# Attention, feed-forward and mixture kernel: transposes of a tile three steps behind its scores, weighted sums eight steps behind

## The chip, the cores and the metric

One core of one Trainium2 chip runs the whole program. The metric is device time in microseconds of one execution; the kernel before takes 1406.84 us (median of 3 runs, 1406.71 to 1406.88).

## The reference

Three stages follow one another; all inputs are float32. Attention has 2 batches of 8 heads, 768 positions of 64 numbers each; a position sees the first 4 positions (the sinks) and the last 128 including itself. The two later stages work on the 1536 x 512 matrix that comes out of it.

```
# attention, for each batch and head
scores = q @ k.T / 8;  scores = where(sink or in window, scores, -1e9)
a = exp(scores - max(scores));  a = a / (a.sum(-1) + 1e-9);  x = a @ v
# feed-forward: d_ff = 2048
h = x @ w_in;  x = (h * sigmoid(h)) @ w_out
# mixture: 8 experts of 1024, P from eight row and column normalisations
P = sinkhorn(exp(x @ w_gate - max));  out = sum_e P[:, e] * (relu(x @ w1[e]) @ w2[e])
```

## The kernel before

Every large product is made of three passes over high and low parts of the operands (`three`, lines 110 to 113): high by high, high by low, low by high. A high part is a copy in the matmul's number format, made by ScalarE (or GpSimd for the values); the low part is what it leaves, made by a subtraction on VectorE or GpSimd.

The attention stage is the function `banded`. Two heads of a batch form a unit; there are 8 units. A unit has 6 query tiles of 128 positions, so there are 48 tiles, numbered s. Three tiles form a window w of 384 positions, of which there are 16. The instructions are issued in the order that the loop over steps writes out (line 325), and each engine works through its own in this order. The loop has 57 steps, numbered s; ii is the step's place in its group of three. In step s the loop issues, in this order:

- `scores(s)`: for two heads, queries by keys on TensorE (L236) into one bank of PSUM each, out of three; on VectorE the mask, and the negative row maximum in one operation (L240). In the first 8 steps four transposes without use follow (L96).
- `exponentials(s - 1)`: for two heads on ScalarE (L248), with the row sums. The results lie in one of 7 buffers `pr`.
- one part of `weighted`: three parts make up a window's sums, values by transposed tiles in three passes (L111 to L113), the first part also with the sinks' high values (L292), the last with their low ones (L302). A part has 6 matmuls of 256 columns, or 12 (first part of a unit's second window). The last part's sum is split into `xH` and `xL`, the input of the next stage.
- `normalise(s - 2)`: on VectorE an addition to the sums (L253), then, behind the low parts (L313) of what the step before had transposed or summed, the reciprocal (L255); on GpSimd two multiplications of the tile by it, one for each head (L257).
- `turn(s - 4)`: two or four transposes of the normalised tile on TensorE (L270), into one of three banks; when ii is 0, `turn_sinks(w - 2)`: three more for a window's sinks (L280).
- high parts of what the step transposed or summed, on ScalarE (L308).
- one piece of the split of the unit's values on GpSimd (`values`, L222 and L224), the loads of later units, and then one step of the generator `timeline` (line 992).

The generator `timeline` brings work of the next stage into these steps: the first weight blocks, which come as 64-bit floating-point numbers, are decoded in eight halves (lines 527 to 555: on ScalarE L535, L545 and L554, on VectorE L540, L541 and L543, on GpSimd L536, L547, L548 and L555). Once the 48 scores are issued it puts blocks of the first layer (twelve matmuls of 512 columns, `first`, lines 626 to 640) into some of the nine last steps: steps 48 to 51 and 54 to 56. The blocks from step 54 on need the sums of window 14. The remaining blocks follow the loop.

Of the kernel before, what the change touches and what calls it, by code (L numbers as in the profile page):

```python
# [26 lines left out]
def attn_ffn_moe_kernel(ctx, tc, q, k, v, n_sink, window, w_in, w_out, w_gate, w1, w2, out):  # L27
# [3 lines left out]
    NT = S // 128  # L31
# [19 lines left out]
    NU = len(units)  # L51
# [42 lines left out]
    def warm_up(ps, n):  # L94
        for _ in range(n):
            nc.tensor.transpose(ps[:, 0:128], ident, ident)  # L96
# [13 lines left out]
    def three(ps, sH, sL, mH, mL, first, last, **kw):  # L110
        nc.tensor.matmul(ps, sH, mH, start=first, stop=False, **kw)  # L111
        nc.tensor.matmul(ps, sH, mL, start=False, stop=False, **kw)  # L112
        nc.tensor.matmul(ps, sL, mH, start=False, stop=last, **kw)  # L113
# [35 lines left out]
    def banded(sp, experts):  # L149
# [36 lines left out]
        def masks():  # L186
            nc.vector.tensor_scalar(kp[:, prev], it[:, prev], wd, None, ALU.is_lt)
            nc.vector.tensor_scalar(mk[:, 1, own], kp[:, own], -1.0, -NEG, ALU.add, ALU.mult)
            nc.vector.tensor_tensor(mk[:, 1, prev], kp[:, prev], snk, ALU.max)
            yield  # L190
            nc.vector.tensor_scalar(mk[:, 1, prev], mk[:, 1, prev], -1.0, -NEG, ALU.add, ALU.mult)
            yield
            nc.vector.tensor_copy(kp[:, 128 : 128 + SK], snk[:, 0:SK])
            nc.vector.tensor_scalar(mk[:, 2], kp, -1.0, -NEG, ALU.add, ALU.mult)
# [49 lines left out]
        def exponentials(s):  # L244
            pr = prs[s % 7]
            sm = sp.small.tile([128, 2], F32, name=f"sm{s}", tag="sm")
            for h, (ng, nm) in enumerate(logits.pop(s)):
                nc.scalar.activation(pr[:, :, h], ng, AF.Exp, bias=nm, scale=-1.0, accum_out=sm[:, h : h + 1])  # L248
            probs[s] = (pr, sm)
# [9 lines left out]
        def turn(s):  # L259

            i = s % NT
            g = i // 3
            pr = probs[s][0]
            js = [(0, 0)] if i == 0 else [(i - 1, 0), (i, 160)]
            n = len(js)
            ps = sp.bank(f"tp{s}", "tr")
            for h in range(2):
                for m, (j, k0) in enumerate(js):
                    o = 128 * (n * h + m)
                    nc.tensor.transpose(ps[:, o : o + 128], pr[:, k0 : k0 + 128, h], ident)  # L270
            ws = [where[j, i] for j, _ in js]
            d = slice(ws[0], ws[-1] + 1, max(ws[-1] - ws[0], 1))
            return [(pt[g][0][:, :, d], pt[g][1][:, :, d], ps[:, : 256 * n].rearrange("p (h m c) -> p h m c", h=2, m=n))]

        def turn_sinks(w):
            ss = sss[w % 2]
            ps = sp.bank(f"ts{w}", "tr")
            for ii in range(3):
                pr = probs.pop(3 * w + ii)[0]
                nc.tensor.transpose(ps[:64, 128 * ii : 128 * ii + 128], pr[:, 128:160, :].rearrange("p s h -> p (s h)"), ident)  # L280
            sinks[w] = ss
            return [(ss[0:64], ss[64:128], ps[0:64, :384])]

        def weighted(w, part):

            u, g = divmod(w, 2)
            b, hp = units[u]
            pH, pL = pt[g]
            ms = [[[0], [1], [2]], [[0, 1], [2], [3]]][g][part]
            if part == 0:  # L290
                pos[w] = sp.bank(f"pv{w}", "pv")[:, :384]
                nc.tensor.matmul(pos[w], vs[0][:, u], sinks[w], start=True, stop=False)  # L292
            po = pos[w]
            for m in ms:
                j, t0 = prods[g][m]
                for h in range(2):
                    vH, vL = (x[:, j, 64 * h : 64 * h + 128] for x in vz[u % 2])
                    mH, mL = (x[:, h, 2 * m : 2 * m + 2].rearrange("p a b -> p (a b)") for x in (pH, pL))
                    three(po[:, 128 * t0 : 128 * t0 + 256], vH, vL, mH, mL, False, False, skip_group_check=True)
            if part < 2:  # L300
                return []
            nc.tensor.matmul(po, vs[1][:, u], sinks.pop(w), start=False, stop=True)  # L302
            c = slice(b * S + 384 * g, b * S + 384 * g + 384)
            return [(xH[hp][:, c], xL[hp][:, c], pos.pop(w))]
# [6 lines left out]
        def lows(parts):  # L311
            for o, l, i in parts:
                nc.vector.tensor_tensor(l, i, f32(o), ALU.subtract)  # L313
# [7 lines left out]
        NS = NT * NU  # L321
        late = []
        vals = iter(())
        setup = masks()
        for s in range(NS + 9):
            w, ii = divmod(s, 3)
            parts, late = late, []
            if s < NS:
                scores(s)
            if s < 8:  # L330
                warm_up(sp.bank("wt", "tr"), 4)
            next(setup, None)
            next(setup, None)
            if 0 <= s - 1 < NS:
                exponentials(s - 1)
            if s >= 9:
                late += weighted((s - 9) // 3, ii)
            nrm = normalise(s - 2) if 0 <= s - 2 < NS else iter(())
            next(nrm, None)
            lows(parts)  # L340
            next(nrm, None)
            if 0 <= s - 4 < NS:
                late += turn(s - 4)
            if ii == 0 and 0 <= w - 2 < 2 * NU:
                late += turn_sinks(w - 2)
            highs(late)
            if s >= NS:
                lows(late)
                late = []
            if s in (3, 4):  # L350
                c = slice(4 * s - 12, 4 * s - 8)
                nc.scalar.copy(vs[0][:, c], vsr[:, c])
                nc.gpsimd.tensor_tensor(vs[1][:, c], vsr[:, c], f32(vs[0][:, c]), ALU.subtract)
            if (s == 4 or s > 2 and s % 6 == 2) and s // 6 < NU:
                vals = values(s // 6)
            next(vals, None)
            if s % 6 == 0 and 0 < s and s // 6 + 1 < NU:
                load_unit(s // 6 + 1, "kq")
            if (s == 8 or s > 5 and s % 6 == 5) and s // 6 + 2 - (s == 8) < NU:
                load_unit(s // 6 + 2 - (s == 8), "v")  # L360
            next(experts)
# [611 lines left out]
    with tc.If(rvl != 0) as cmp:  # L973
        with tc.manual_schedule(), ExitStack() as st:
            sp = Space(st)
            ex = Experts(sp)
            ex.plan(True)

            halves = [words(sp.vsr, 512 * i, 512) for i in range(2)]
            tmp = [[words(sp.tm, 512 * i + 256 * c, 256) for c in range(2)] for i in range(2)]  # L980

            def load_half(i):
                c = 256 * (i // 2)
                nc.sync.dma_start(halves[i % 2].bitcast(I32).rearrange("p (k f) -> p k f", k=2), w_in.bitcast(I32)[:, c : c + 256].rearrange("(k p) f -> p k f", p=128)[:, 2 * (i % 2) : 2 * (i % 2) + 2])

            def decode_half(i):
                o = [words(t, 256 * (i % 2), 256, F32R) for t in ex.buffer("A", 0, i // 2)]
                yield from ex.decode(halves[i % 2], tmp[i % 2], o, True)
                if i + 2 < 8:
                    load_half(i + 2)  # L990

            def timeline():
                gens = {}
                for s in range(NT * NU + 9):
                    if s == 5:
                        load_half(0)
                        load_half(1)
                    for i in range(8):
                        at = s - 7 - 5 * i
                        if at == 0:  # L1000
                            gens[i] = decode_half(i)
                        if at in (0, 1, 2, 3, 4, 5, 6):
                            next(gens[i], None)
                    at = s - NT * NU
                    for a in (-6, -1, -1, 0):
                        if at == a:
                            ex.fetch()
                    if at == -3:
                        gens["Z"] = ex.prepare("Z", 0, 0)
                    if -3 <= at <= 1:  # L1010
                        next(gens["Z"], None)
                    if at in (0, 1, 2, 3, 6, 7, 8):
                        next(blocks)
                    yield

            blocks = ex.run(True)
            banded(sp, timeline())
            sp.cycle = ["sc"] * 3 + ["tr"] * 3
            for _ in blocks:
                pass  # L1020
# [51 lines left out]
```

## Time and profile before

| | before |
|---|---|
| median of 3 runs | 1406.84 us |
| profiled execution, its own time | 1406.43 us |
| its span, first to last instruction | 1404.5 us |
| busy: TensorE, VectorE, ScalarE, GpSimd | 1394.5, 850.8, 538.2, 504.3 us |
| granted TensorE clock, mean | 0.999 |
| attention stage, scores of the first to those of the last tile | 8.59 to 118.10 us |

The profile records one execution. The table's busy times are unions of the instructions' durations; those of matmuls overlap and their ends are modelled, so the distance between starts says more than a duration. The stage around the change is the first tenth of the span; the two later stages take the rest, in which TensorE is busy nearly all the time.

### The profile page before, as it was taken

The page shows a single profiled execution, that of the slowest core. Times are in us where ns is not written, and L with a number is a line of the kernel's source. Part 1 is how long each engine was busy: PE and PEld are TensorE (multiplying, and loading weights), DVE is VectorE, ACT ScalarE, POOL GpSimd, SP SyncE. Part 2 cuts the span into 40 slices and gives each one's busy share as a digit, 9 for nine tenths or more (in the row PEclk, how much of TensorE's full clock was granted, in tenths as well). Part 3 has the DMA queues.
Part 4 walks back from the last instruction along what each step waited for, and adds up shares of the span by engine and source line. Part 5 has one row for each costly group of instructions (what it writes and reads, how often), then busy time and mean ns, then how long its engine had stood idle before and what let it go on. Part 6 is the DMA issues. An engine that isn't in the chain of part 4 may idle for free.

```text
span 1404.5 us, 18978 instructions
## 1 busy us (share of the span) xinstructions
PE 1394.5 (99%) x7065; PEld 1221.5 (87%) x7065; DVE 850.8 (61%) x1645; ACT 538.2 (38%) x1241; POOL 504.3 (36%) x657
## 2 busy tenths in 40 slices
PE   8999999999999999999999999999999999999998
PEld 6778888888878998889989998998899889989997
DVE  7988897686566656554555455455545554555454
ACT  6887334333354333333333333333233333332330
POOL 7887232222133333433332234323322333232230
PEclk9999999999999999999999999999999999999999
DMA  5341221211001000011001001100100010001002
GB/s 133 110 129 67 70 83 65 69 60 61 16 25 36 31 31 31 30 45 31 31 31 45 30 31 32 44 31 31 46 31 30 31 45 30 31 31 46 16 0 93
DMA packets 60293, 65.29 MB, mean 46 GB/s; under 512 B 10400, under 2 KB 47520, under 8 KB 60192
## 3 DMA queue, kind: packets, MB, share of 16 engines
q1 hardware_dynamic: 59904, 63.99, 14.3%
q8 instruction: 57, 0.93, 0.3%
q14 instruction: 44, 0.36, 0.1%
q10 hardware_dynamic: 288, 0.00, 0.0%
HBM read 60.84 MB, written 3.15 MB: 46 GB/s over the span
## 4 chain that ended last, share of the span: by engine, by line
PE 97%; POOL 1%; DVE 1%; DMA 1%; SPq 0%; ACT 0%; issue 0%; ACTq 0%; DVEq 0%
PE py L112 12%; PE py L113 12%; PE py L111 12%; PE pq L111 11%; PE pq L113 11%; PE pq L112 11%; PE pz L112 3%; PE pz L111 3%; PE pz L113 3%; PE pa L112 3%; PE pa L113 3%; PE pa L111 3%; PE sc L236 2%; PE tp L270 1%; PE pv L111 1%; PE pv L113 1%
## 5 line engine op out<-in xcount | busy, mean ns | idle before, releaser
L834 DVE SCALAR_TENSOR_TENSOR pr<-py,P,pr 128x512 f32<-128x512 f32 x224 | 168.0, 750 | 117.9 <-PE py L113 117.9
L113 PE MATMUL py<-pt,vz 128*128 128x512 f32 x576 | 225.4, 391 | 0.0
L112 PE MATMUL py<-pt,vz 128*128 128x512 f32 x576 | 225.3, 391 | 0.0
L111 PE MATMUL py<-pt,vz 128*128 128x512 f32 x576 | 224.8, 390 | 0.3 <-DVE ngm L886 0.3
L787 DVE TENSOR_TENSOR mk<-pq,rqk 128x384 f32<-128x384 f32 x128 | 71.3, 557 | 205.3 <-PE pq L113 205.3
L571 POOL TENSOR_TENSOR pt<-ng,pt 128x256 fp32r<-128x256 f32 (+1 forms) x66 | 66.4, 1011 | 211.3 <-ACT pt L570 211.3
L571 POOL TENSOR_TENSOR pt<-rqk,pt 128x512 fp32r<-128x512 f32 (+1 forms) x50 | 55.4, 1108 | 225.1 <-ACT pt L570 225.1
L113 PEld LDWEIGHTS py<-pt,vz 128*128 128x128 f32 x576 | 108.1, 188 | 22.8
L111 PEld LDWEIGHTS py<-pt,vz 128*128 128x128 f32 x576 | 108.1, 188 | 20.7 <-DVE ngm L886 0.3
L112 PEld LDWEIGHTS py<-pt,vz 128*128 128x128 f32 x576 | 108.1, 188 | 19.9
L794 ACT COPY rqk<-pq 128x384 f32<-128x384 f32 x64 | 30.7, 480 | 216.4 <-PE pq L113 216.4
L790 ACT ACTIVATE vz<-mk 128x384 fp32r<-128x384 f32 x128 | 66.9, 522 | 80.0 <-DVE mk L787 80.0
L791 DVE SCALAR_TENSOR_TENSOR vz<-mk,vz 128x384 fp32r<-128x384 f32 x128 | 71.0, 554 | 7.7 <-ACT vz L790 7.7
L112 PE MATMUL py<-pt,ss 128*128 128x512 f32 x192 | 74.9, 390 | 0.0
L111 PE MATMUL py<-pt,ss 128*128 128x512 f32 x192 | 74.6, 389 | 0.0
L636 ACT ACTIVATE mk<-pa 128x512 f32<-128x512 f32 x48 | 28.7, 599 | 89.8 <-PE pa L113 82.1
L834 DVE SCALAR_TENSOR_TENSOR tm<-py,P,tm 128x512 f32<-128x512 f32 x56 | 42.0, 751 | 32.6 <-PE py L113 32.6
L637 DVE TENSOR_TENSOR mk<-mk,pa 128x512 f32<-128x512 f32 x48 | 32.9, 685 | 41.6 <-ACT mk L636 41.6
L570 ACT CAST pt<-ng 128x256 fp32r<-128x256 f32 (+1 forms) x66 | 33.5, 509 | 63.2 <-POOL ng L585 24.9
L257 POOL TENSOR_SCALAR pr<-pr,sm 128x288 f32<-128x288 f32 x96 | 52.1, 560 | 15.4 <-DVE sm L255 6.6
L111 PE MATMUL pa<-xH,wa 128*128 128x512 f32 x144 | 56.4, 392 | 0.0
L112 PE MATMUL pa<-xL,wa 128*128 128x512 f32 x144 | 56.2, 390 | 0.3 <-DVE xL L313 0.3
(428 smaller groups left out, 3799.9 us busy)
## 6 DMA issues: line engine op xcount, KB each, us to landing
rqk<-in_moe_w_dram SPq DMA_DIRECT2D x32, 512.0 KB, 3.3
rv<-in_moe_w_dram SPq DMA_DIRECT2D x16, 512.0 KB, 3.4
ng<-in_moe_w_dram SPq DMA_DIRECT2D x16, 512.0 KB, 3.2
rqk<-in_moe_w_out_dram SPq DMA_DIRECT2D x8, 512.0 KB, 3.3
rv<-in_v_dram SPq DMA_DIRECT2D x8, 384.0 KB, 3.8
rqk<-in_moe_w_in_dram SPq DMA_DIRECT2D x6, 512.0 KB, 3.8
rqk<-in_k_dram SPq DMA_DIRECT2D x7, 384.0 KB, 4.7
rqk<-in_q_dram SPq DMA_DIRECT2D x7, 384.0 KB, 5.1
```

Source lines behind the costliest of these rows:

```text
L111: nc.tensor.matmul(ps, sH, mH, start=first, stop=False, **kw)
L112: nc.tensor.matmul(ps, sH, mL, start=False, stop=False, **kw)
L113: nc.tensor.matmul(ps, sL, mH, start=False, stop=last, **kw)
L257: nc.gpsimd.tensor_scalar(pr[:, :, h], pr[:, :, h], sm[:, h : h + 1], 1.0, ALU.mult, ALU.mult)
L570: nc.scalar.copy(o[0], src)
L571: nc.gpsimd.tensor_tensor(o[1], src, f32(o[0]), ALU.subtract)
L637: nc.vector.tensor_tensor(sg, sg, ps, ALU.mult)
L787: add = lambda o, x, y: nc.vector.tensor_tensor(o, x, y, ALU.add)
L790: nc.scalar.activation(oH, src, AF.Relu)
L791: nc.vector.scalar_tensor_tensor(oL, src, 0.0, f32(oH), ALU.max, ALU.subtract)
L794: nc.scalar.copy(self.p1, ps)
L834: nc.vector.scalar_tensor_tensor(o, ps, self.P[:, tt, e : e + 1], o, ALU.mult, ALU.add)
```

## The change

In the loop over steps the transposes of a tile are issued one step earlier relative to its scores, those of a window's sinks too (in the last step of a group of three, with the window before it, where they stood in the first with the window two before), and the three parts of the weighted sums begin eight steps behind a window's first scores, where they began nine behind. Normalisation keeps its step. The loop has one step less, and `timeline` too; the last three blocks of the first layer that are issued inside it move from the seventh, eighth and ninth of the last steps to the sixth, seventh and eighth.

```diff
-        for s in range(NS + 9):
+        for s in range(NS + 8):
...
-            if s >= 9:
-                late += weighted((s - 9) // 3, ii)
+            if s >= 8:
+                late += weighted(*divmod(s - 8, 3))
             nrm = normalise(s - 2) if 0 <= s - 2 < NS else iter(())
             next(nrm, None)
             lows(parts)
             next(nrm, None)
-            if 0 <= s - 4 < NS:
-                late += turn(s - 4)
-            if ii == 0 and 0 <= w - 2 < 2 * NU:
-                late += turn_sinks(w - 2)
+            if 0 <= s - 3 < NS:
+                late += turn(s - 3)
+            if ii == 2 and 0 <= w - 1 < 2 * NU:
+                late += turn_sinks(w - 1)
...
-                for s in range(NT * NU + 9):
+                for s in range(NT * NU + 8):
...
-                    if at in (0, 1, 2, 3, 6, 7, 8):
+                    if at in (0, 1, 2, 3, 5, 6, 7):
                         next(blocks)
```

## Rows read from the trace of the kernel before

**Rows 1.** Busy time by stretch: per engine, then clock, DMA share, GB/s.
```profile
8.00:28.00 20.00, 18.91 (x113) 11.96 (x111) 17.61 (x73) 13.89 (x45) 16.59 (x33) 1.00 0.67 168
28.00:118.00 90.00, 90.00 (x608) 69.07 (x605) 81.30 (x305) 76.27 (x232) 76.42 (x130) 1.00 0.35 100
```

**Rows 2.** Timeline of TensorE: start us, duration us, engine, line, operation, operands.
```profile
35.65 0.76 PE L236 MATMUL sc<-rqk 64*128 64x288 f32 x4
...
37.72 0.76 PE L236 MATMUL sc<-rqk 64*128 64x288 f32 x4
...
61.47 0.76 PE L236 MATMUL sc<-rqk 64*128 64x288 f32 x4
...
63.87 0.65 PE L270 MATMUL tp<-ident,pr 128*128 128x128 f32 x4
...
64.77 0.76 PE L236 MATMUL sc<-rqk 64*128 64x288 f32 x4
...
66.28 0.64 PE L270 MATMUL tp<-ident,pr 128*128 128x128 f32 x4
66.85 0.76 PE L236 MATMUL sc<-rqk 64*128 64x288 f32 x4
...
69.08 0.76 PE L236 MATMUL sc<-rqk 64*128 64x288 f32 x4
...
71.67 0.76 PE L236 MATMUL sc<-rqk 64*128 64x288 f32 x4
...
73.50 0.76 PE L236 MATMUL sc<-rqk 64*128 64x288 f32 x4
...
75.74 0.76 PE L236 MATMUL sc<-rqk 64*128 64x288 f32 x4
...
117.34 0.76 PE L236 MATMUL sc<-rqk 64*128 64x288 f32 x4
```

**Rows 3.** Timeline of GpSimd, same columns; in brackets idle time before and its releaser.
```profile
36.71 1.05 POOL L257 TENSOR_SCALAR pr<-pr,sm 128x288 f32<-128x288 f32 x2
...
38.89 1.05 POOL L257 TENSOR_SCALAR pr<-pr,sm 128x288 f32<-128x288 f32 x2 [0.65 <-DVE sm L255]
...
63.98 1.15 POOL L257 TENSOR_SCALAR pr<-pr,sm 128x288 f32<-128x288 f32 x2
...
66.23 0.73 POOL L555 TENSOR_TENSOR wa<-tm,wa 128x256 fp32r<-128x256 f32 x1
66.94 1.03 POOL L257 TENSOR_SCALAR pr<-pr,sm 128x288 f32<-128x288 f32 x2
...
76.08 1.30 POOL L257 TENSOR_SCALAR pr<-pr,sm 128x288 f32<-128x288 f32 x2
...
116.82 1.03 POOL L257 TENSOR_SCALAR pr<-pr,sm 128x288 f32<-128x288 f32 x2 [1.32 <-DVE sm L255]
...
123.25 1.03 POOL L257 TENSOR_SCALAR pr<-pr,sm 128x288 f32<-128x288 f32 x2
```

**Rows 4.** Timeline of VectorE in the step that begins at 35.65 us.
```profile
36.43 0.46 DVE L240 CUSTOM_DVE_ANT_0 ng<-sc,mk 128x288 f32<-128x288 f32 x1 [1.04 <-PE sc L236]
...
37.26 0.69 DVE L313 TENSOR_TENSOR pt<-tp,pt 128x512 fp32r<-128x512 f32 x1
37.98 0.55 DVE L313 TENSOR_TENSOR ss<-ts,ss 64x384 fp32r<-64x384 f32 x1
38.56 0.17 DVE L255 RECIPROCAL sm<-sm 128x2 f32<-128x2 f32 x1
```

**Rows 5.** Line L253, 28 to 118 us: ns minimum/median/maximum; and one of its instructions.
```profile
L253 DVE TENSOR_SCALAR sm<-sm x37: 158/243/715, 29.8 to 117.5; 128x2 f32<-128x2 f32 x37
...
66.32 0.67 DVE L253 TENSOR_SCALAR sm<-sm 128x2 f32<-128x2 f32 x1
```

**Rows 6.** Chain that ended last, 10 to 30 us: start us, us, what.
```profile
26.10 0.98 POOL vz L224
...
28.33 0.69 PE sc L236 x4
```

**Rows 7.** Waits of TensorE: line, releaser, total us, times, longest us.
```profile
PE pa L112 <- DVE xL L313: 0.3, 1, 0.3
```

## The prediction

> **What bounds the kernel now.** I read the busy times by stretch first, then the engines one by one in order of time, then the list of who waited for whom. From 28 to 118 us, the body of the attention stage, TensorE is busy for all of the 90 us, VectorE for 81, ScalarE and GpSimd for 76 each, at a granted clock of 1.00 [rows 1]. So TensorE sets the pace and the other three follow with little to spare. The six steps from 61.47 to 75.74 us take 3.30, 2.08, 2.23, 2.58, 1.84 and 2.23 us, 14.27 together, measured from one tile's scores to the next [rows 2]. TensorE's work per tile is the same before and after, so a shorter pipeline can only win where TensorE idles now; and it loses if TensorE must wait for a tile that arrives later than its new place.
>
> What arrives is the normalised tile. For tile s the chain is: scores, the masked maximum on VectorE (L240), exponentials on ScalarE, in step s+2 the sum's small addition and reciprocal on VectorE (L253, L255), the two multiplications on GpSimd (L257), then the transposes on TensorE. Today they stand at the end of step s+4, after the change at the end of step s+3, just ahead of the scores of tile s+4.
>
> **The body.** Take tile 21. Its multiplications begin at 63.98 us [rows 3]; a head's takes about half of the pair's duration, so the first head is ready at 64.51. Today's transposes of it start at 66.28 and the next scores at 66.85 [rows 2]: they take 0.57, and there is 1.8 us of slack. In the new order they precede the scores of tile 25, now at 64.77, so their place is 64.20: 0.31 us too early. Tile 22 is ready at 66.94 + 0.52 = 67.46, its new place is 66.85 - 0.57 = 66.28: 1.2 us. Tile 26 is ready at 76.08 + 0.65 = 76.73; with it go the three transposes of the sinks, which together with its own take 0.90 (as from 63.87 to 64.77), so its place is 75.74 - 0.90 = 74.84 and it lacks 1.9, the most of all [rows 2, 3]. I did this for tiles 10 (36.71 + 0.53 against 37.72 - 0.57: 0.09) to 43 (116.82 + 0.53 against 117.34 - 0.57: 0.58), 34 tiles: 24 of them come too late, and these 24 deficits add up to 18.6 us.
>
> How much of the sum is paid depends on whether a wait of TensorE delays the next tiles too. The row that decides is VectorE's. The scores of tile 13 start at 35.65, L240 at 36.43, 0.78 later, having waited for them [rows 4]; the reciprocal for tile 11 follows behind L240 and two low parts (0.69 and 0.55) and ends at 38.73; GpSimd waited 0.65 us for it, starts at 38.89 and is done at 39.94 [rows 3, 4]. That is 4.29 us from the scores of tile 13 to the readiness of tile 11, every link waiting for the one before. In the new order the transposes of tile 11 come ahead of the scores of tile 15: with the second head's half of 0.57 and a release like the 0.16 between reciprocal and GpSimd, some 0.45, the loop over two steps costs at least 4.7 to 4.8 us. The steps above make pairs of 5.38, 4.31, 4.81, 4.42, 4.07 and 5.53: three of six are shorter, so they are stretched even when nothing queues. And GpSimd does queue: from the scores of tile 24 at 61.47 to the end of tile 22's multiplications at 67.97 is 6.5 us, since a decode addition (L555, 66.23) stood in front [rows 2, 3].
>
> So both ends of the body's cost: if GpSimd and VectorE keep today's times whatever TensorE does, TensorE falls behind once by the largest deficit, 1.9 us, and then everything fits. If they shift with it one for one, all 18.6 are paid. L240 began within 0.93 us of its scores' start, as in rows 4, for about half of the tiles from 10 to 45 (those shift with TensorE); for the others VectorE was late from its own queue and can catch up. I take half: 9.3 us.
>
> L253 lies in that loop, and it is no fixed term: a 128x2 operation, it takes 158 ns at least, 243 in the median and up to 715, and the one from 66.32 to 66.99 ended with GpSimd's L555, which ran from 66.23 to 66.96 [rows 3, 5]. The Trainium skill, page "SBUF — State Buffer", section "Who interferes with whom", says that a VectorE operation in a two-port mode, as a tensor-scalar one can be, and a GpSimd operation share a port pair under an exclusive lock, and that the later one is fully blocked; this row agrees. By the rule a tighter loop meets GpSimd's work at least as often, and the median's 0.09 us above the minimum would come on top once per two steps, 19 times: an estimate of 1.7 us, and 1418.9 in place of the sum below. I leave it out of the sum.
>
> **The fill.** The body begins when TensorE stops waiting. Today the first weighted sums stand in step 9 and wait for the last part of the first unit's values, which GpSimd makes from 26.10 to 27.08; the scores of step 10 start at 28.33 in the chain of waits [rows 6]. After the change these sums stand in step 8, but that GpSimd operation is issued in step 7 as before, behind the multiplications of tile 5, and comes no sooner. By 28.3 TensorE has then done the same transposes and sums and one score pair less, 0.69 us: the gain of starting one step earlier is lost. It would be worth at best the work of that first part, about 1.0 us; at worst tile 5 is itself late by the scores of tile 7, which now wait for tile 3, some 1.1 us more. I take +0.7, ends -1.0 and +1.8.
>
> **The drain.** One step is gone, but it holds no idle time: the sums of that step are still done, and the first-layer blocks between them move with them. The one stall seen there, 0.3 us for the low part of the last-but-one window [rows 7], keeps its distance of one group and may go or stay. New is tile 45: its multiplications start at 123.25 [rows 3] behind decode work on GpSimd, and its transposes move from step 49, behind a whole block of twelve matmuls, to step 48, some 0.7 us after the 120.6 at which the sums and transposes of step 47 end in today's time: 2.4 us of wait if GpSimd is no earlier. Since TensorE has already fallen behind by then, I take +1.0 and -0.2 for the stall: +0.8, ends -0.3 and +2.4.
>
> Queues passed: no DMA is issued by the moved calls. The loads of keys, queries and values, the decode steps and the weight fetches keep their step numbers, all before step 49; only the last three blocks are one step earlier, behind the same group of sums. Instruction counts do not change on any engine; the banks used by transposes are freed in the same order. I cost these at nothing.
>
> **Sum.** 9.3 + 0.7 + 0.8 = 10.8 us over the profiled execution's own 1406.43 us (span 1404.5 and 1.9 around it): 1417.2. The median of the runs shown is 0.4 above that execution, so 1417.6, rounded to 1417.5. The ends: 1.9 - 1.0 - 0.3 = +0.6 and 18.6 + 1.8 + 2.4 = +22.8.
>
> **Rivals.**
> First, not slower: GpSimd and VectorE run on their own queues. Then TensorE falls behind once and the rest fits. For it: for about half of the tiles VectorE was late from its own queue. Against it: the row with four links waiting in a chain. Price 1.9 in the body, decided at the point where scores-to-ready falls under about 4.1 us; with the fill at its best (-1.0) and the stall gone (-0.3) 1407.4, and if the deficits vanish altogether 1405.5; within 0.2% of before either way. Chance 0.18.
>
> Second, everything shifts: all deficits are paid and the drain waits in full, 1406.8 + 22.8 = 1429.6. For it: step lengths below the loop's floor. Against it: TensorE's waits let GpSimd's queue run empty, and rows like 38.89 show it idle. Chance 0.08.
>
> Third, the clock: TensorE's waits lower the granted clock for a stretch. It stayed at 1.00, its 2.4 GHz level, from 8 to 28 us, where TensorE was busy for 18.91 of 20, and in the body [rows 1]. At 1.2 GHz for a quarter of the body the 90 us would grow by 22: 1440 with the rest. The Trainium skill, page "TensorE: Matmul & The Clock Gate", section "HAM oscillation — how this bites in real kernels", warns of this for idle gaps; no run here shows it. My waits are under 2 us each with work between. Chance 0.03.
>
> Fourth, a faster kernel by over 0.2%, 2.8 us: under 1404: the fill and drain at their best give 1.3, and the rest would need idle time in the body, where TensorE shows none. Chance 0.04.
>
> **How the numbers follow.** Forecast, 1410 to 1425, 0.67; the rivals 0.18, 0.08, 0.03, 0.04. Below 1408 lie the first rival's share and the fourth, some 0.15; above 1425 about 0.1. Range 1407.5 to 1425. A measurement here tells about 0.2% from no change: slower by more 0.78, within 0.18, faster 0.04.
>
> **What would show it.** Right: in the profile after, waits of the transposes (L270) for the multiplications on GpSimd (L257), six steps of the body at 15 to 16 us, most scores-to-ready times at 4.1 to 5 us, GpSimd idling more before L257, and the time from 144 us on shifted but not changed in length. Wrong: six steps still at 14.3 to 14.5, or waits named for something else, such as the score banks or the transposes' banks.

## The result, and the profile after

The changed kernel takes 1422.05 us (median of 4 runs, 1421.21 to 1422.84), the kernel before 1406.86 on the same chip: a ratio of 1.0108, 95% interval 1.0096 to 1.0120. That is 15.2 us slower. The forecast was 1417.5, range 1407.5 to 1425. The profiled execution has a span of 1420.0 us against 1404.5, so 15.5 us are to be found in it.

Busy time by stretch in the kernel after, columns as in [rows 1]:
```profile
8.00:28.00 20.00, 18.12 (x102) 11.01 (x100) 14.84 (x63) 12.87 (x40) 15.70 (x31) 1.00 0.66 168
28.00:118.00 90.00, 86.39 (x543) 63.09 (x544) 75.46 (x275) 68.13 (x208) 67.57 (x115) 1.00 0.34 96
```
In the same 90 us of the body TensorE issues 543 matmuls where it issued 608, 11% fewer, at an unchanged clock of 1.00. Its busy time falls by 4% only: per matmul it grew from 0.148 to 0.159 us, since a matmul that waits is shown longer (four transposes that waited are shown with 1.00 us below, four that did not with 0.65 in [rows 2]). The count per stretch tells the loss better here than the busy share does. All other engines do less work in the 90 us as well, so none of them has become the bound by its load.

Waits of TensorE after (line, releaser: total us, times, longest us):
```profile
PE tp L270 <- POOL pr L257: 6.3, 13, 1.3
PE pa L112 <- DVE xL L313: 1.0, 1, 1.0
```
The first wait, of the transposes for the multiplications on GpSimd, was 0.2 us once in the whole kernel before. The second was 0.3 [rows 7].

These are the waits of the matmuls alone. PEld is the loading of an operand into TensorE ahead of its matmul, which the profile lists by itself; for the transposes, from 28 to 130 us:
```profile
PEld tp L270 <- POOL pr L257: 10.0, 29, 1.0
```
The same list of the kernel before has none from 28 to 118 us. Loading overlaps matmuls (in [rows 1] TensorE is busy with matmuls for all of 90 us, and loading is the second entry, 69.07), so the 10.0 us need not be lost in full, but they are near the body's loss below, which the 6.3 us alone would not explain.

Points of equal work split the 15.5 us. TensorE before, the first sums after the last scores and the first matmul behind the first layer's blocks:
```profile
119.40 0.42 PE L292 MATMUL pv<-ss,vs 128*128 128x384 f32 x1
...
153.48 0.39 PE L111 MATMUL pz<-kt,zq 128*128 128x512 f32 x1
```
TensorE after, one of the first scores, one group of six steps, and the same two points:
```profile
29.38 0.76 PE L236 MATMUL sc<-rqk 64*128 64x288 f32 x4
...
70.14 0.76 PE L236 MATMUL sc<-rqk 64*128 64x288 f32 x4
...
72.22 0.76 PE L236 MATMUL sc<-rqk 64*128 64x288 f32 x4
...
74.82 1.00 PE L270 MATMUL tp<-ident,pr 128*128 128x128 f32 x4 [0.77 <-POOL pr L257]
75.76 0.76 PE L236 MATMUL sc<-rqk 64*128 64x288 f32 x4
...
78.33 0.76 PE L236 MATMUL sc<-rqk 64*128 64x288 f32 x4
80.18 0.76 PE L236 MATMUL sc<-rqk 64*128 64x288 f32 x4
...
82.42 1.00 PE L270 MATMUL tp<-ident,pr 128*128 128x128 f32 x4 [0.40 <-POOL pr L257]
83.35 0.76 PE L236 MATMUL sc<-rqk 64*128 64x288 f32 x4
...
86.66 0.76 PE L236 MATMUL sc<-rqk 64*128 64x288 f32 x4
...
132.38 0.45 PE L292 MATMUL pv<-ss,vs 128*128 128x384 f32 x1
...
169.00 0.39 PE L111 MATMUL pz<-kt,zq 128*128 128x512 f32 x1
```
- Fill. The scores at 29.38 are those of step 9. With a pair of them (0.69) done, TensorE stands at 30.07, where before it stood at 28.26 before step 10 (28.33 in the chain of [rows 6]): +1.8.
- Body. 132.38 against 119.40 is +12.98, of which the fill had 1.8: +11.2. The six steps from 70.14 take 2.08, 3.54, 2.57, 1.85, 3.17 and 3.31 us, 16.52 together; those of [rows 2] took 14.27. From the scores of tile 12 to those of tile 42 the mean of six steps is 16.23 after and 14.48 before.
- Drain. 169.00 against 153.48 is +15.52: another +2.5.
- The rest, from that matmul behind the first layer's blocks to the end of the span: 1251.0 in both.

### The profile page after: what moved, and what is told of

Read it like the earlier page. It is cut to its first block, busy times and chain, and to the rows that moved or that the text cites. A ratio compares the mean times of both kernels' runs of the same rounds, so it can differ in the third digit from the quotient of the medians.

```text
span 1420.0 us, 18975 instructions
## 1 busy us (share of the span) xinstructions
PE 1403.1 (99%) x7065; PEld 1223.2 (86%) x7065; DVE 851.8 (60%) x1645; ACT 539.0 (38%) x1241; POOL 502.5 (35%) x657
## 4 chain that ended last, share of the span: by engine, by line
PE 94%; POOL 2%; DVE 1%; DMA 1%; issue 1%; SPq 0%; ACT 0%; ACTq 0%; POOLq 0%; DVEq 0%
PE py L112 12%; PE py L113 12%; PE py L111 12%; PE pq L111 11%; PE pq L113 11%; PE pq L112 11%; PE pz L111 3%; PE pz L113 3%; PE pz L112 3%; PE pa L112 3%; PE pa L113 3%; PE pa L111 3%; PE tp L270 2%; PE sc L236 1%; POOL pr L257 1%; PE pv L111 1%
## 5 line engine op out<-in xcount | busy, mean ns | idle before, releaser
L257 POOL TENSOR_SCALAR pr<-pr,sm 128x288 f32<-128x288 f32 x96 | 51.5, 552 | 30.1 <-DVE sm L255 14.9
```

The lines of the kernel that those rows point to most:

```text
L257: nc.gpsimd.tensor_scalar(pr[:, :, h], pr[:, :, h], sm[:, h : h + 1], 1.0, ALU.mult, ALU.mult)
```

## The experiments

All ratios are against the kernel before on the same chip, with 95% intervals; "slower by" is the difference of the medians. The kernel before took 1406.77 to 1406.94 us (medians) wherever it ran beside these kernels, so their medians can be compared with each other.

**The transposes alone, and the sums alone.** The change moves two things; each was done by itself. In the first kernel only the transposes move:
```diff
-            if 0 <= s - 4 < NS:
-                late += turn(s - 4)
-            if ii == 0 and 0 <= w - 2 < 2 * NU:
-                late += turn_sinks(w - 2)
+            if 0 <= s - 3 < NS:
+                late += turn(s - 3)
+            if ii == 2 and 0 <= w - 1 < 2 * NU:
+                late += turn_sinks(w - 1)
```


> Transposes three steps behind, weighted sums left at nine (57 steps). Loop theory: the loss comes from TensorE waiting at the transposes for the normalised tile, whatever the sums do, so nearly all of the 15.2 us is here: 1419 to 1424 us, six steps of the body at 16.0 to 16.6 us. Rival, the sums: the earlier weighted sums wait for parts that are not ready or crowd the low parts on VectorE; then this kernel is at 1405 to 1409.

Measured: 1424.99, ratio 1.0127 (1.0110 to 1.0144), slower by 18, one microsecond above the expected range. In the second only the sums move:
```diff
-        for s in range(NS + 9):
+        for s in range(NS + 8):
...
-            if s >= 9:
-                late += weighted((s - 9) // 3, ii)
+            if s >= 8:
+                late += weighted(*divmod(s - 8, 3))
...
-                for s in range(NT * NU + 9):
+                for s in range(NT * NU + 8):
...
-                    if at in (0, 1, 2, 3, 6, 7, 8):
+                    if at in (0, 1, 2, 3, 5, 6, 7):
```


> Transposes left at four steps, weighted sums at eight (56 steps). Loop theory: the slack of the transposes stays, so 1405.5 to 1408 us, with at most 1 us won or lost at the fill, where the first sums wait for GpSimd's values. Rival, the sums: most of the loss is here, 1415 to 1422.

Measured: 1414.76, ratio 1.0058 (1.0041 to 1.0074), slower by 7.8. The first kernel confirms that the transposes carry the loss without the sums. It is even slower than the changed kernel, and its VectorE shows a reason: three low parts, of the window (xL), the tile (pt) and the sinks (ss), now fall in one step and all stand ahead of the reciprocal.
```profile
62.03 0.55 DVE L313 TENSOR_TENSOR xL<-pv,xH 128x384 fp32r<-128x384 f32 x1
62.49 0.68 DVE L313 TENSOR_TENSOR pt<-tp,pt 128x512 fp32r<-128x512 f32 x1
63.20 0.55 DVE L313 TENSOR_TENSOR ss<-ts,ss 64x384 fp32r<-64x384 f32 x1
63.79 0.17 DVE L255 RECIPROCAL sm<-sm 128x2 f32<-128x2 f32 x1
```
The second kernel missed its expectation: the sums alone lose as well, though no tile is transposed earlier. Its waits of TensorE show where, and its sums (TensorE) one of them:
```profile
PE pv L292 <- DVE ss L313: 6.0, 9, 1.2
...
64.61 0.44 PE L292 MATMUL pv<-ss,vs 128*128 128x384 f32 x1 [0.40 <-DVE ss L313]
```
The sums' first matmul (L292) reads the sinks' low part, which VectorE makes at 64.00 to 64.55, in the step after their transposes. From the transposes of a window's first tile to its sums there are five steps before, five after, and four here; from those of its sinks, which come with its last tile, three, three and two.

**One step more for the transposes.** This kernel was put on record together with the two above, to see whether a longer distance wins anything. In hindsight it tests the second one: transposes at five behind their scores with sums still at nine leave four steps between them too, though every tile is ready long before.
```diff
-            if 0 <= s - 4 < NS:
-                late += turn(s - 4)
-            if ii == 0 and 0 <= w - 2 < 2 * NU:
+            if 0 <= s - 5 < NS:
+                late += turn(s - 5)
+            if ii == 1 and 0 <= w - 2 < 2 * NU:
```


> Transposes five steps behind, sums at nine. Loop theory: at four steps the slack is already enough, so nothing is left to win in the body, 1405.5 to 1408.5. Rival, a smooth trade in which every step of distance is worth about the same: 1390 to 1400.

Measured: 1418.35, ratio 1.0085 (1.0068 to 1.0101), slower by 11.4. The expectation was missed by far, and the same wait is there, larger:
```profile
PE pv L292 <- DVE ss L313: 10.3, 11, 4.0
```

**Five and five.** Transposes five steps behind and sums ten: both distances are then long enough (the loads and fetches that keep pace with them are shifted too).
```diff
-        for s in range(NS + 9):
+        for s in range(NS + 10):
...
-            if s >= 9:
-                late += weighted((s - 9) // 3, ii)
+            if s >= 10:
+                late += weighted(*divmod(s - 10, 3))
...
-            if 0 <= s - 4 < NS:
-                late += turn(s - 4)
-            if ii == 0 and 0 <= w - 2 < 2 * NU:
+            if 0 <= s - 5 < NS:
+                late += turn(s - 5)
+            if ii == 1 and 0 <= w - 2 < 2 * NU:
...
```


> Transposes five steps behind and sums ten (58 steps; the split of the values, their loads and one weight fetch move one step later with them). Two-gap theory: a loss comes when scores-to-transposes falls under four steps (wait for GpSimd) or transposes-to-sums under five (the sums' first matmul waits for the low part of the sinks, as in the kernels with 4/8 and 5/9). Here the gaps are 5 and 5, so neither wait appears in the body: 1405.5 to 1410, six steps at 14.3 to 14.9. Rival: five steps before the transposes is itself slow (ScalarE or the score buffers held longer): 1415 to 1420.

Measured: 1411.48, ratio 1.0032 (1.0021 to 1.0044), slower by 4.7. The body came out as expected, six steps in 14.26 to 15.07. The total is above the expected range; one wait in the drain, again for the sinks' low part (L313), here behind decode work on VectorE, goes with it:
```profile
142.17 0.69 PE L292 MATMUL pv<-ss,vs 128*128 128x384 f32 x1 [3.16 <-DVE ss L313]
```

**Sums at eight, the sinks' parts made first.** The sums alone, as above, but ScalarE and VectorE make the sinks' high and low parts ahead of the tile's own. Against the kernel with the sums alone:
```diff
-            if 0 <= s - 4 < NS:
-                late += turn(s - 4)
+            own = turn(s - 4) if 0 <= s - 4 < NS else []
             if ii == 0 and 0 <= w - 2 < 2 * NU:
                 late += turn_sinks(w - 2)
+            late += own
```


> Transposes four and sums eight steps behind, as before in that pair, but the high and low parts of a window's sinks are made ahead of those of the step's tile. Theory of the second gap: the sums' first matmul waits for the low part of the sinks, which now comes some 0.7 us earlier, once in three steps, 16 windows: the 7.9 us over the kernel before shrink to 1.5 to 5, 1408 to 1412. If something else in that pair costs, 1413.5 to 1416.

Measured: 1409.3, ratio 1.0018 (1.0009 to 1.0027), slower by 2.4. The wait of L292 is gone from TensorE's list; its timeline has the sums of the same window at 64.71 without a bracket:
```profile
64.71 0.44 PE L292 MATMUL pv<-ss,vs 128*128 128x384 f32 x1
```
Six steps take 14.26 to 14.39. So four steps do suffice between transposes and sums once the order on VectorE fits: 5.5 of the 7.8 us of the sums alone (1414.76 to 1409.3) went with this wait. What is left lies in the fill of the profiled execution, in part by the clock, which fell there (last section).

**No decode.** The body's loss with the decode work, which queues on GpSimd and VectorE, taken out: its operations are left out and two scaled copies on ScalarE put in their place.
```diff
-                yield from ex.decode(halves[i % 2], tmp[i % 2], o, True)
+                rw = halves[i % 2].rearrange("p (m w) -> p m w", w=2)
+                for _ in range(6):
+                    yield
+                nc.scalar.activation(o[0], rw[:, :, 0].bitcast(U32), AF.Copy, scale=2.0**-37)
+                nc.scalar.activation(o[1], rw[:, :, 0].bitcast(U32), AF.Copy, scale=2.0**-50)
```


> The changed kernel without the decode of the first weight block inside the attention stage: left out are its operations on VectorE and GpSimd; ScalarE only scales the raw words into both parts, so these weights are not the reference's. If the body's 11 us are the bare loop over two steps, which is over the pairs of steps by itself, six steps stay at 15.0 to 15.4 and the time is 1411 to 1416. If they are the queue of decode work in front of the tiles, six steps fall to 14.3 to 14.6 and the time to 1406 to 1410. If decode has no part, nothing changes: 1420 to 1423.

Measured: 1418.86, ratio 1.0084 (1.0067 to 1.0101), slower by 12.1. With GpSimd busy for 51.0 of the 90 us from 28 on, where it was 67.6, six steps still take 15.96 to 16.06 (from tile 12 on), nearly the 16.23 of the changed kernel. The time lies between the ranges expected for the bare loop and for no part of decode: the loop was taken too short. Most of the loss is no queue: in all of the eleven loops from 40 to 121 us that set the pace, GpSimd had stood idle for 1.55 or 1.59 us when the multiplications began. It is the loop itself. Its links, over two steps, on TensorE, VectorE and GpSimd of this kernel:
```profile
85.22 0.76 PE L236 MATMUL sc<-rqk 64*128 64x288 f32 x4
...
87.30 0.76 PE L236 MATMUL sc<-rqk 64*128 64x288 f32 x4
...
89.37 1.02 PE L270 MATMUL tp<-ident,pr 128*128 128x128 f32 x4 [0.23 <-POOL pr L257]
90.32 0.76 PE L236 MATMUL sc<-rqk 64*128 64x288 f32 x4
```
```profile
78.44 0.44 DVE L253 TENSOR_SCALAR sm<-sm 128x2 f32<-128x2 f32 x1
...
86.01 0.46 DVE L240 CUSTOM_DVE_ANT_0 ng<-sc,mk 128x288 f32<-128x288 f32 x1 [0.99 <-PE sc L236]
...
86.77 0.45 DVE L253 TENSOR_SCALAR sm<-sm 128x2 f32<-128x2 f32 x1
87.14 0.68 DVE L313 TENSOR_TENSOR pt<-tp,pt 128x512 fp32r<-128x512 f32 x1
87.85 0.55 DVE L313 TENSOR_TENSOR ss<-ts,ss 64x384 fp32r<-64x384 f32 x1
88.43 0.17 DVE L255 RECIPROCAL sm<-sm 128x2 f32<-128x2 f32 x1
```
```profile
78.34 0.51 POOL L222 TENSOR_SCALAR vz<-rv 128x384 fp32r<-128x384 f32 x1
...
86.17 1.03 POOL L224 TENSOR_TENSOR vz<-rv,vz 128x384 fp32r<-128x384 f32 x1
...
88.79 1.03 POOL L257 TENSOR_SCALAR pr<-pr,sm 128x288 f32<-128x288 f32 x2 [1.59 <-PE pv L113]
```
(The last bracket names a matmul; the reciprocal, which this operation reads, ended at 88.60.) Scores at 85.22, masked maximum at 86.01, L253 at 86.77, two low parts, reciprocal at 88.43, multiplications at 88.79, transposes at 89.37, next-but-one scores at 90.32: 5.10 us, with VectorE nearly without a gap from 86.01 to 88.6. Of the 5.10, L253 has 0.45; it ends with GpSimd's L224, and its like at 78.44, in the other pair of these six steps that is stretched (5.05), with L222. In the kernel before, in the chain of [rows 4], it took 0.17:
```profile
37.19 0.17 DVE L253 TENSOR_SCALAR sm<-sm 128x2 f32<-128x2 f32 x1
```
With that in place of 0.45 the loop is 4.82.

**The reciprocal first.** If the loop sets the body's pace, moving the two low parts (some 1.2 us) behind the reciprocal must give it back. Changed kernel, with one line moved:
```diff
             next(nrm, None)
-            lows(parts)
             next(nrm, None)
+            lows(parts)
```


> The changed kernel with the reciprocal issued ahead of the low parts on VectorE instead of behind them. Loop theory: the loop over two steps loses 0.7 to 1.3 us of low parts and falls from 4.7 or more to some 3.6 to 4.1, below nearly every pair of steps (4.1 to 5.5), so most of the body's 11 us comes back: 1408 to 1413, six steps at 14.4 to 15. Rival, GpSimd's own queue sets the pace of the normalised tiles: the reciprocal's place hardly matters, 1418 to 1422.

Measured: 1415.67, ratio 1.0062 (1.0045 to 1.0079), slower by 8.7: 6.4 of the 15.2 us are back (1422.05 to 1415.67), less than expected. Its waits of TensorE:
```profile
PE tp L270 <- POOL pr L257: 1.5, 2, 0.9
...
PE sc L236 <- DVE nm L240: 1.4, 4, 0.5
```
The transposes hardly wait any more, but the scores now wait for the masked maximum (L240) of an older tile. Six steps still take 15.5 in most of the body (15.32 in the mean from tile 12 to 42, where the kernel before has 14.48).

**Without the small addition L253.** L253 was left out of the changed kernel, of the kernel before, and of the one with the reciprocal first (later lines have numbers one lower):
```diff
-            nc.vector.tensor_scalar(sm, sm, 1.0e-9, None, ALU.add)
```


> The changed kernel without the addition of 1e-9 to the row sums (L253; a sum is at least 1, so in float32 the result is the same). Loop theory with the block: of the two pairs of steps that are over length in each six, one has L253 held up for 0.45 us by GpSimd's L224 and the other pays 0.16 or more, so six steps fall by 0.5 to 0.9 us from 16.3 and the time to 1416 to 1419. Rival, the operation is worth its bare 0.16 us twice in six steps, some 2 us in all: 1419.5 to 1421. If VectorE is not in the loop: 1421.5 to 1422.5.

> The kernel before without that addition, 4 steps and 9. Both theories of the gaps: there is no wait of the transposes to shorten, only some 1.6 us of score pairs that wait for VectorE in the body and a stall of 0.3 in the drain, so 1405 to 1406.8. If VectorE's load were what sets the pace, 48 times 0.28 us would show: 1393 to 1400.

> The changed kernel with the reciprocal ahead of the low parts and without the addition. If what is left of the loss with the reciprocal first (1415.7) is VectorE arriving late at the scores' banks, 0.28 us less work per tile on it shows: 1411 to 1414. If it is fill and drain alone, 1415 to 1416.

Measured: 1417.0 (1.0073, 1.0059 to 1.0086) from the changed kernel, 5.05 us less; 1405.64 (0.9992, 0.9983 to 1.0001, 11 runs) from the kernel before, 1.2 us less, with an interval that just holds 1; 1411.52 (1.0036, 1.0022 to 1.0050) with the reciprocal first, 4.15 us less. All three lie in the first of their ranges. So this operation costs 3.85 us more in the shorter pipeline than in the longer one. With both remedies six steps mostly take 14.27 to 14.84, as before the change, and 4.65 us of the 15.2 are left. The kernel before without L253 has the lowest median of all that ran, though not one clear of the kernel before.

**Fill and drain by themselves.** The kernel before with the short distance only for the first eight tiles, and only for the last six (in these the sums stay nine behind):
```diff
-            if 0 <= s - 4 < NS:
-                late += turn(s - 4)
-            if ii == 0 and 0 <= w - 2 < 2 * NU:
-                late += turn_sinks(w - 2)
+            turns = [s - 3] if s - 3 < 8 else [s - 4] if s - 4 >= 8 else []
+            for r in turns:
+                if 0 <= r < NS:
+                    late += turn(r)
+                    if r % 3 == 2:
+                        late += turn_sinks(r // 3)
```
```diff
+            turns = [s - 4] if s - 4 < 42 else []
+            turns += [s - 3] if s - 3 >= 42 else []
...
```


> The kernel before, with only the transposes of tiles 0 to 7 three steps behind; the rest four, sums at nine. This is the fill's share alone. By the trace of the changed kernel it is 1.8 us (scores of step 9 at 29.38 plus one score pair of 0.69, against 28.26 for step 10 before): 1408 to 1409.5. If the fill were hidden by what follows, 1406.5 to 1407.5; the prediction's own term was 0.7.

> The kernel before, with only the transposes of tiles 42 to 47 three steps behind; the rest four, sums at nine. The drain's share alone: one wait of some 1.3 to 2.4 us for tile 45 behind the decode work on GpSimd, and no more: 1408 to 1409.5. If that wait only stood in for a later one, 1406.5 to 1407.5.

Measured: fill 1408.84, ratio 1.0016 (1.0006 to 1.0025), slower by 2.1, as expected; drain 1409.84, ratio 1.0020 (1.0010 to 1.0029), slower by 3.1, slightly over. The drain's waits were not those I had in mind:
```profile
117.86 0.48 PE L270 MATMUL tp<-ident,pr 128*128 128x128 f32 x2 [1.16 <-DVE sm L255]
...
120.73 0.71 PE L270 MATMUL tp<-ident,pr 128*128 128x128 f32 x4 [0.79 <-POOL rqk L539]
```
They belong to the first tiles that are moved, 42 and 43, where the order switches: one step there has the transposes of two tiles and of a window's sinks, three banks, which is all that the transposes have. The tiles themselves were ready 1.7 us before (GpSimd was done with them at 116.16 and 118.98), and each wait ends 0.14 to 0.15 us after the low parts of the tile that had the bank before; the operations that the brackets name end about then too. VectorE:
```profile
117.04 0.68 DVE L313 TENSOR_TENSOR pt<-tp,pt 128x512 fp32r<-128x512 f32 x1
...
119.90 0.68 DVE L313 TENSOR_TENSOR pt<-tp,pt 128x512 fp32r<-128x512 f32 x1
```
So they are best read as waits for banks, made by this experiment's own switch, and tile 45 waits only 0.27 us here. The 3.1 us neither isolate nor bound the drain's share; that they lie near the expectation is luck. The drain rests on the trace of the changed kernel alone.

## Why the prediction was right, step by step

The sign, the mechanism and the place were right: 1422.05 lies in the range, and slower had 0.78. The forecast is 4.55 us low, and each of its three terms was mis-sized downwards.

**Body, 9.3 forecast, 11.2 found.** The signs that the prediction named are there: the L270 waits, steps a little longer than the 15 to 16 named (16.2), scores-to-ready at 4.62 us in the mean (4.05 to 5.76), and GpSimd idle before L257 for 23.1 us (28 to 130 us) against 11.6 before (28 to 118). In the kernel before, scores-to-ready was 5.08 in the mean, longer than after, since tiles stood in queues more. Within this term two steps failed.
- "I leave it out of the sum": L253 beside GpSimd. The loop was forecast at 4.7 to 4.8 us at least; it is 5.05 to 5.10 in the kernel without decode, and 4.82 with L253 at its undisturbed length. The forecast set 0.09 us in each of 19 loops beside the sum. Found are 0.28 in each loop that sets the pace, two in six steps and so twelve in the body, which makes 3.4 us. The changed kernel itself shows it too: of its twelve such pairs of steps from 37.7 to 131.7 us, the four with L253 at 0.17 or 0.18 last 4.92 in the mean, the eight with 0.37 to 0.74 last 5.19. Taking the operation out altogether should give twelve times 0.45, 5.4; it gave 5.05 in the whole kernel, of which some 4.0 lie in the body (the mean of six steps falls from 16.23 to 15.57). In the changed kernel L253 lasts 355 ns in the median, 243 before [rows 5]:
```profile
L253 DVE TENSOR_SCALAR sm<-sm x38: 158/355/741, 27.7 to 128.5; 128x2 f32<-128x2 f32 x38
```
The rule behind that estimate is in the Trainium skill, page "SBUF — State Buffer", section "Who interferes with whom", and the trace agrees with it at both places shown in the kernel without decode, where L253 ends with GpSimd's operation.
- "I take half: 9.3", because VectorE and GpSimd would catch up from their own queues for the other half. The size was near, the reason was wrong: without the decode queue most of the loss stays (12.1 of 15.2 in all). What limits the sum is that only some pairs of steps are shorter than the loop: two of six, where the prediction counted three. The third, 4.42, kept its length (75.76 to 80.18 after); it ends in a tile with two transposes in place of four, and L253 took 0.16 in it. A sum by the loop would have been: the pairs of 4.31 and 4.07 lack 0.79 and 1.03 of 5.10, together 1.82 in six steps, 10.9 in the body's six such groups, where 11.2 was found. With the 4.75 of the forecast it would have been 6.7, so the half covered what the missing L253 took away; that 9.3 came within 2 us of 11.2 is luck.

**Fill, 0.7 forecast with ends -1.0 and +1.8; 1.8 found.** It stands at the upper end, and by what the upper end named, tile 5 itself late. GpSimd after:
```profile
26.19 1.03 POOL L257 TENSOR_SCALAR pr<-pr,sm 128x288 f32<-128x288 f32 x2
27.16 1.02 POOL L224 TENSOR_TENSOR vz<-rv,vz 128x384 fp32r<-128x384 f32 x1
```
The multiplications of tile 5 start at 26.19, and behind them the last part of the values at 27.16, 1.1 later than the 26.10 of [rows 6]. That it "comes no sooner" was right; the 0.7 assumed that it comes no later either. The first delay comes earlier than the prediction's wait for tile 3 (0.15): a wait of 1.18 at tile 2, whose multiplications (19.36) stand behind another GpSimd operation (L353, 18.11 to 19.39). The kernel with the short distance in the fill alone gives 2.1.

**Drain, 0.8 forecast with ends -0.3 and +2.4; 2.5 found.** Tile 45's wait of +1.0 was right: TensorE (first line) waits 1.26 for GpSimd (the other two), which is behind decode work as foreseen.
```profile
137.04 1.01 PE L270 MATMUL tp<-ident,pr 128*128 128x128 f32 x4 [1.26 <-POOL pr L257]
```
```profile
135.25 0.80 POOL L548 TENSOR_TENSOR tm<-tm 128x256 f32<-128x256 f32 x1
136.03 1.46 POOL L257 TENSOR_SCALAR pr<-pr,sm 128x288 f32<-128x288 f32 x2
```
The stall for the low part of a window, which "may go or stay" and was taken as -0.2, grew from 0.3 to 1.0. These two make some 2.0 of the 2.5. Another 0.37 is in tile 45's transposes, which take 0.77 to the next matmul after their wait (137.04 to 137.81), where they took 0.40 before (125.38 to 125.78).

**The edits costed at nothing.** The rest of the kernel takes 1251.0 us in both, and the sums at eight cost nothing in the changed kernel, since transposes and sums moved together: with the sums left at nine it is 2.9 us slower. That they could cost 7.8 us alone was not seen.

**The rivals.** The first, that GpSimd and VectorE keep their own pace, had a price of 1.9 us in the body and falls with the 11.2 found; in the kernel without decode, where GpSimd has no queue in front of the tiles that matter, the body still loses nearly as much. The second, everything shifts, stands 7.5 us above the result. The third, the clock, did not occur in the changed kernel; no run showed it when the prediction was written, but three of the experiments do (last section). The fourth, a faster kernel, is excluded by the interval.

What stays open is why the reciprocal first, with L253 still in place, gives back only 6.4 us; its new wait on L240 is seen, but was not taken apart further than by removing L253.

## What to carry to other kernels

In a pipeline whose engines each work in a written order, every distance between stages can have a floor: add up the chain of links from one tile's scores to the place that waits for it, tiny operations and those ahead in each queue included, and set it against the sum of the steps it spans, shortest spans first. An engine that is busy for all of its time says nothing about this. A lighter load on the others gave back little here (3.2 of 15.2 us without decode), the order within a step more (6.4 with the reciprocal first). When two distances share a budget, as four plus five steps here, check the second one too: taking a step from either of them by itself cost 7.8 us or more.

## What the runs showed of the hardware

TensorE's granted clock fell to its lower level in the profiled executions of three experiments, twice after one long wait and once after a half-busy stretch with two shorter ones, and not in the changed kernel, whose waits at the transposes are at most 1.3 us. With transposes at five and sums at ten (columns as in [rows 1]):
```profile
138.00:142.00 4.00, 1.01 (x9) 0.75 (x7) 3.87 (x7) 0.75 (x2) 0.14 (x1) 1.00 0.00 0
142.00:145.50 3.50, 3.33 (x14) 3.33 (x15) 0.68 (x2) 0.00 (x0) 0.00 (x0) 0.52 0.00 0
145.50:149.00 3.50, 3.50 (x19) 2.96 (x19) 0.01 (x1) 0.65 (x2) 0.00 (x0) 0.99 0.00 0
```
TensorE did 1.01 us of work in four, at 1.00; then the clock is at 0.52, near its 1.2 GHz level, for 3.5 us of nearly full work, and back at 0.99. With transposes at five and sums at nine it was so from 148.58 to 151.99 us, after the wait of 4.0. With the sums at eight and the sinks first it was in the fill:
```profile
24.00:27.00 3.00, 1.45 (x8) 0.88 (x6) 1.93 (x9) 1.94 (x8) 3.00 (x6) 0.99 0.99 260
27.00:30.00 3.00, 2.72 (x10) 1.64 (x10) 0.00 (x0) 1.25 (x4) 2.11 (x5) 0.50 0.45 126
30.00:33.00 3.00, 3.00 (x15) 2.54 (x15) 2.20 (x9) 0.39 (x2) 1.22 (x3) 0.50 0.07 19
```
Half-busy from 24 to 27, with waits of 0.38 and 1.45, then 0.50 for six microseconds of nearly full work. A group of scores (L236) takes 1.33 us there, against 0.76 at the full clock. Its eleven executions differ by this: the six with a mean clock of 0.999 or 1.000 took 1407.3 to 1409.3 us, the five with 0.997 or 0.998 took 1410.1 to 1411.2. A wait thus cost more than its own length where the clock fell; that it was the wait that lowered the clock was not tested by itself.
